# Preparing combined weights on another engine, and sooner, in a fused attention and two-FFN kernel

## The chip, the cores and the metric

The kernel runs on one core of a Trainium2 chip. The metric is the device time of one launch in microseconds (us), the median of three runs. Details come from one further execution that was taken with the hardware profiler.

## What is computed

Three stages follow each other, and the tokens of all four batches are handled as one list of 2304.

```python
# q, k, v: 4 batches, 8 heads, 576 positions, 64 wide
scores = (q @ k.T) / 8 * Dmat          # Dmat[i, j] = gamma_h ** (i - j) for i >= j, else 0
x = scores @ v                         # 2304 x 512
h = x @ w_in                           # 512 -> 2048
g = maximum(h, 0) + alpha * minimum(h, 0)
x = g @ w_out                          # 2048 -> 512
gate = 1 / (1 + exp(-(x @ w_gate)))    # 512 -> 1536
out = (gate * (x @ w_val)) @ w_out2    # 1536 -> 512
```

The weights arrive as 64-bit floating point words; the kernel turns them into 32-bit numbers itself.

## The kernel before

**Products.** Each 32-bit operand is split into a high part (rounded to the fp32r type that TensorE takes) and a low rest, and a product is the sum of three matmuls: high by high, high by low, low by high (`products`, L634 is its matmul). Splitting is a copy on ScalarE and a subtraction on VectorE (`split`, L201 and L202).

**Blocks and stages.** The tokens are cut into blocks of 256, 512, 512, 512 and 512 (j = 0 to 4). TensorE's instructions keep the order in which the program writes them. The other engines' order, and that of the DMA queue on SyncE (SP), which issues every transfer, is made by a planner that simulates the program and places an instruction when the simulation has it ready; `behind` only keeps some work behind marked urgent instructions. Once built, every engine and the queue work strictly by that list.

1. To about 156 us: attention of blocks 0 and 1 with the first FFN on them. The weights of each of the 16 feature chunks f are loaded, made single and split (`prepare_weight`), and written back to HBM; chunks below `RES` stay in SBUF until block 2 has used them, later ones are fetched again (`fetch`, L268).
2. 156 to about 327 us: the loop at the end of the program with j = 1 (its chunks 11 to 15) and j = 2 (chunks 0 to 15), called steps here. Each step is `ffn1_h` (12 matmuls of 512 columns; then ScalarE forms the positive part and the negative part, L648 and L649, VectorE joins them, L650, and `split` follows), and one step later `ffn1_y`. The h results lie in a ring of two PSUM banks (`ps_h`), free again only after the split on VectorE. Between them run the attention of blocks 2 to 4, chunk of tokens by chunk (`att_stages`: scores, a mask on VectorE at L519, values; GpSimd scales the next chunk's q and v, L497 and L505), and preparations of the second FFN's weights.
3. 327 to about 410 us: blocks 3 and 4 together in four double steps (`h_step`). Two chunks and their partners eight chunks on are computed with seven half-size products instead of eight. This needs combinations of the tokens (`seven`, tiles `xx_1` to `xx_7`, made in `left_factors(-1)` during the last steps of j = 2) and of the weights: the **sums**, `prepare_sums(t)` for t = 0 to 7, two for each double step. `leaky` (L760, L761, L763) makes the activation of a double step.
4. 410 to 505 us: `y_phase`. From there to the end the second FFN runs in the same seven-product form, then block 0 in plain form.

**Preparations.** A list `jobs` holds 18 preparations of the second FFN's weights (`prepare_quarters`). One loads two raw tiles, makes them single (ScalarE L224, L225; VectorE L228, L230, L233), combines quarters on GpSimd (L300), splits them (ScalarE L310, VectorE L311) and writes them to HBM. `ask` loads the raw tiles of the next one, if two of five raw slots are free; `begin_job` starts it; `second_pace(n)` adds n to a count in each step of the loop, asks at one half and begins at one. `second_step` moves every running preparation on by one piece. `begin_job((1, t))` puts a sum at the head of the list; but if some other preparation is already asked for, that one is started and the sum waits for the next call. In the program before, step 12 of j = 2 calls it for sum 0 with a preparation asked for.

A sum reads the tile `b` (two weight tiles written to HBM earlier, L367) and is three subtractions on GpSimd (L336: one of 128 x 512, two of 128 x 256), a copy on ScalarE (L344) and a subtraction on VectorE (L346).

**SBUF.** Everything else lies in 38 slots of 4 KB per partition, handed out in the order in which they came free: 5 are raw slots, the other 33 hold weights, activations, attention chunks (a q and k slot, a k and v slot) and the halves of preparations. In step 12 of j = 2 seven of them are set aside for the weights of the double steps (`load_inner`).

Of the kernel before, what the change touches and what calls it, by code (L numbers as in the profile page):

```python
# [10 lines left out]
F32 = mybir.dt.float32  # L11
# [4 lines left out]
ALU = mybir.AluOpType  # L16
# [3 lines left out]
P = 128  # L20
# [3 lines left out]
DM = 512  # L24
KC = DM // P
NF1 = 2048 // P
# [17 lines left out]
PLAIN = 3  # L44
# [1 line left out]
NIN = NSUM // 2  # L46


RES = 10


EARLY, LATE = 2, 5
# [1 line left out]
BESIDE = 11  # L54
# [9 lines left out]

PACE_S, PACE_Y = 0.33, 0.5


SPAN_X = 21  # L70


def chunks():
# [39 lines left out]
def retention_two_ffn(ctx: ExitStack, tc: tile.TileContext, att, cst, alpha, w1, w2, out0, out1):  # L113
    nc = tc.nc
# [217 lines left out]
    def prepare_sums(t):  # L332

        b, s = raw_w.pop((1, t))
        b21, b22 = b[:, 0, DM // 2:], b[:, 1, DM // 2:]
        sub = lambda o, a, b: nc.gpsimd.tensor_tensor(out=o, in0=a, in1=b, op=ALU.subtract)  # L336
        sub(s[:, 0:2], b[:, 1].rearrange("p (k j) -> p k j", k=2), b[:, :, :DM // 2])
        yield
        sub(s[:, 2], b22, s[:, 0])
        sub(s[:, 3], b21, s[:, 2])  # L340
        free(b)
        yield
        w = [slot([P, 4, DM // 2], F32R, f"s{t}{x}", quarter_slots) for x in "hl"]
        nc.scalar.activation(w[0], s, AF.Copy)  # L344
        yield
        nc.vector.tensor_tensor(out=w[1], in0=s, in1=w[0].bitcast(F32), op=ALU.subtract)  # L346
        free(s)
        inner[t // 2, t % 2, 0] = w
# [5 lines left out]
    asked = []  # L354
# [12 lines left out]
                nc.sync.dma_start(out=b, in_=w1f[t])  # L367

    def begin_job(*now):
        jobs[:0] = now  # L370
        ask()
        if asked:
            job = asked.pop()
            second.append((job, (prepare_sums, prepare_quarters)[job[0] - 1](*job[1:])))
# [19 lines left out]
    def second_pace(n):  # L394
        second_step()
        due[0] += n
        if due[0] >= 1.0:
            due[0] -= 1.0
            begin_job()
        elif due[0] >= 0.5:  # L400
            ask()
# [34 lines left out]
    def weight_step(n):  # L436

        credit[0] += n
        if credit[0] >= 1.0:
            credit[0] -= 1.0  # L440
            begin_weight()
        advance()
# [4 lines left out]
    o = 0  # L447
# [4 lines left out]
    def load_chunk(n):  # L452
        if n >= len(CHUNKS) or n in raw_a:
            return
        load_qk(n)
        load_kv(n)

    def load_qk(n):
        if n >= len(CHUNKS):
            return  # L460
        c = CHUNKS[n][3]
        half = 2 * c * H * D
        qk = slot([P, 2, NPAIR, P], F32, f"qk{n}")
        a = offset[n]
        src = att[a:a + half].rearrange("(p t a i) -> p t a i", p=P, t=2, a=NPAIR)
        if n == 0:
            nc.sync.dma_start(out=c_sb, in_=cst)
            nc.sync.dma_start(out=qk[:, :, 0:2, :c], in_=src[:, :, 0:2])
            nc.sync.dma_start(out=qk[:, :, 2:4, :c], in_=src[:, :, 2:4])
        else:  # L470
            nc.sync.dma_start(out=qk[:, :, :, :c], in_=src)
        raw_a[n] = [qk, None]

    def load_kv(n):
        if n >= len(CHUNKS):
            return
        c = CHUNKS[n][3]
        half = 2 * c * H * D
        kv = slot([P, 2, H * D], F32, f"kv{n}")
        a = offset[n] + half  # L480
        nc.sync.dma_start(out=kv[:c], in_=att[a:a + half].rearrange("(p t d) -> p t d", p=c, t=2))
        raw_a[n][1] = kv

    x_t = {}
    def att_q(n):

        _, _, pos, c, _ = CHUNKS[n]
        by = decay
        if pos:

            by = ap.tile([P, NPAIR, P], F32, tag="dec", name=f"dec{n}", bufs=2)
            for pr in range(NPAIR):
                g = O_GP + STARTS.index(pos) * NPAIR + pr
                nc.scalar.activation(by[:, pr, :c], decay[:, pr, :c], AF.Copy, scale=c_sb[:, g:g + 1])
        for part in (slice(0, 2), slice(2, 4)) if n == 0 else (slice(0, 4),):
            q = raw_a[n][0][:, 0, part, :c]
            nc.gpsimd.tensor_tensor(out=q, in0=q, in1=by[:, part, :c], op=ALU.mult)  # L497
# [83 lines left out]
    def att_stages(j):  # L581

        for n in runs_of(j):
            x_of(n)
            s_sb = att_scores(n, ps_a, "ab")
            load_qk(n + 1)
            yield
            att_values(n, s_sb, ps_a, "ab")
            load_kv(n + 1)
            if n + 1 < len(CHUNKS):  # L590
                att_q(n + 1)
                att_v(n + 1)
            yield
# [78 lines left out]
    def ffn1_y(j, f):  # L672
        w, g = weight(f, 1), g_t.pop((j, f))
        if f == 0:
            if j == 0:
                y_t[j] = [t[:, e] for t in [
                    ps_a.tile([P, 2, BLOCKS[j]], F32, tag=x, name=f"y{j}{x}") for x in "ab"
                ] for e in range(2)]
            else:
                y_t[j] = [ps_y.tile([P, BLOCKS[j]], F32, tag="y", name=f"y{j}_{e}") for e in range(KC)]  # L680
        for e in range(KC):

            products(
                y_t[j][e], [(cols(w, e), g)],
                f == 0 and (j > 0 or e % 2 == 0), f == NF1 - 1 and (j > 0 or e % 2 == 1),
            )
        used(f, 1)
        free(g)
        if f == NF1 - 1:
            for e in range(KC):  # L690
                drain(e, f"yst{j}_{e}", y_t[j][e], x2d[j][:, e, :])
# [64 lines left out]
                yield  # L756

    def leaky(dst, src, f, name):
        t = small.tile([P, DM], F32, tag="t", name=name, bufs=1)
        nc.scalar.activation(t, src, AF.Relu)  # L760
        urgent["act"].append(nc.scalar.activation(src, src, AF.Relu, scale=-1.0))  # L761
        urgent["dve"].append(
            nc.vector.scalar_tensor_tensor(dst, src, na_sb[:, f:f + 1], t, ALU.mult, ALU.add)  # L763
        )
# [397 lines left out]
    for f in range(NF1):  # L1162

        while step1 < EARLY or (step1 - EARLY) * (NF1 - 1) < (BESIDE - EARLY) * f:
            ffn1_h(1, step1)
            weight_step(PACE_C)
            later(BEHIND - 1 if step1 >= EARLY else EARLY)
            late.append((1, step1))
            step1 += 1
            if step1 > EARLY:  # L1170
                break
        ffn1_y(0, f)
        weight_step(PACE_C)
        weight_step(PACE_C)
        if done[0] < NF1:
            ffn1_h(0, done[0])
            done[0] += 1
        weight_step(PACE_C)
        weight_step(PACE_C)
    n = runs_of(2)[0]  # L1180
    load_chunk(n)
    att_q(n)
    att_v(n)
    def stages_of(*js):
# [3 lines left out]
    for j in range(1, PLAIN):  # L1188
        stages = stages_of(2) if j == 1 else stages_of(3, 4)
        first = step1 if j == 1 else 0  # L1190
        total = 2 * sum(len(runs_of(i)) for i in ((2,) if j == 1 else (3, 4)))
        span = SPAN * (NF1 - first) // NF1 if j == 1 else SPAN_X
        staged = 0
        for f in range(first, NF1):
            fetch(f, 0)
            fetch(f + 1, 0)
            fetch(f, 1)
            ffn1_h(j, f)
            second_pace(PACE_S)
            if j == PLAIN - 1 and staged == total:  # L1200
                if not under_left:

                    for _ in stages:
                        pass
                    for x in "ab":
                        ps = ps_a.tile([P, DM], F32, tag=x, name=f"whole{x}")
                        nc.tensor.matmul(ps, wt[f, 1][:, 0, :P], x_t[j][:, 0, 0], start=True, stop=True)
                    att_only.close()
                    pool = ctx.enter_context(tc.tile_pool(name="late", bufs=1, reuse_waits="tile"))
                    spare.extend((pool, f"late{i}") for i in range(NLATE))  # L1210
                    under_left.append(left_factors(-1))
                else:
                    next(under_left[0], None)
            if j == PLAIN - 1 and f == 12:
                quarter_slots.extend(spare.popleft() for _ in range(NQ))
                load_inner(0)
            if j == PLAIN - 1 and f in (12, 13):
                begin_job((1, f - 12))
            for point in range(2):
                second_step()  # L1220
                if staged < total and staged * span < total * (2 * (f - first) + point):
                    next(stages)
                    staged += 1
                if point == 0:
                    later(BEHIND - 1)
                elif under_left:
                    next(under_left[0], None)
            late.append((j, f))
        for _ in stages:
            pass  # L1230
# [168 lines left out]
```

## Time and profile before

| | |
|---|---|
| Median of 3 runs | 904.96 us (903.76 to 906.84) |
| The profiled execution | 906.68 us |
| Its span, first to last instruction | 904.9 us |
| Mean granted clock of TensorE | 0.991 |
| TensorE matmul (PE) busy | 862.4 us, 95% |
| VectorE (DVE) busy | 564.9 us, 62% |
| ScalarE (ACT) busy | 447.4 us, 49% |
| GpSimd (POOL) busy | 152.0 us, 17% |
| Chain that ended last | PE 67%, DVE 13%, DMA 8%, ACT 6%, issue 3%, SP's queue 2%, POOL 1% |

A busy share is time in which an instruction of that engine ran. The chain that ended last is followed back from the last instruction, at each step to what released it. "A <- B" in the lists of waits says that A sat idle until B ended.

### The profile page before, as it was taken

The page shows a single profiled execution, that of the slowest core. Times are in us where ns is not written, and L with a number is a line of the kernel's source. Part 1 is how long each engine was busy: PE and PEld are TensorE (multiplying, and loading weights), DVE is VectorE, ACT ScalarE, POOL GpSimd, SP SyncE. Part 2 cuts the span into 40 slices and gives each one's busy share as a digit, 9 for nine tenths or more (in the row PEclk, how much of TensorE's full clock was granted, in tenths as well). Part 3 has the DMA queues.
Part 4 walks back from the last instruction along what each step waited for, and adds up shares of the span by engine and source line. Part 5 has one row for each costly group of instructions (what it writes and reads, how often), then busy time and mean ns, then how long its engine had stood idle before and what let it go on. Part 6 is the DMA issues. An engine that isn't in the chain of part 4 may idle for free.

```text
span 904.9 us, 13084 instructions
## 1 busy us (share of the span) xinstructions
PE 862.4 (95%) x4770; PEld 719.3 (79%) x4770; DVE 564.9 (62%) x805; ACT 447.4 (49%) x785; POOL 152.0 (17%) x143
## 2 busy tenths in 40 slices
PE   5689989999999989999999999999999999999998
PEld 4578978777778867777788888887888888888897
DVE  2689995475665976776984877358952233497122
ACT  3478884445543675676752655335532322353111
POOL 5100001233621742321440231100000000000000
PEclk9799999999999999999999999999999999999999
DMA  9679998776785845669698799934598554269970
GB/s 296 231 256 352 370 391 319 269 248 245 246 319 212 337 178 177 227 232 339 224 401 338 257 399 418 409 144 163 194 378 334 188 185 163 97 208 349 395 278 24
DMA packets 89392, 244.01 MB, mean 270 GB/s; under 512 B 13040, under 2 KB 16112, under 8 KB 89328
## 3 DMA queue, kind: packets, MB, share of 16 engines
q1 hardware_dynamic: 89328, 243.17, 74.1%
q8 instruction: 38, 0.62, 0.3%
q14 instruction: 26, 0.21, 0.1%
HBM read 174.98 MB, written 68.16 MB: 269 GB/s over the span
## 4 chain that ended last, share of the span: by engine, by line
PE 67%; DVE 13%; DMA 8%; ACT 6%; issue 3%; SPq 2%; POOL 1%; DVEq 0%; ACTq 0%; POOLq 0%
PE a L634 14%; PE oa L634 7%; PE yy L634 7%; PE h L634 5%; PE y L634 5%; PE z L634 4%; PE e L634 4%; PE b L634 4%; PE c L634 3%; PE o L634 2%; PE oc L634 2%; PE ob L634 2%; PE oe L634 2%; DMA kv<-att 2%; PE a_h L634 2%
## 5 line engine op out<-in xcount | busy, mean ns | idle before, releaser
L634 PE MATMUL h<-x,w 128*128 128x512 f32 (+1 forms) x444 | 89.6, 353 | 5.8 <-DVE g L202 4.3
L634 PEld LDWEIGHTS h<-x,w 128*128 128x128 f32 x444 | 71.0, 192 | 18.1 <-DVE g L202 5.7
L300 POOL TENSOR_TENSOR r<-r,r 128x256 f32<-128x256 f32 x36 | 43.2, 1206 | 165.7 <-DVE r L233 111.6
L311 DVE TENSOR_TENSOR q<-r,q 128x512 fp32r<-128x512 f32 x72 | 54.2, 783 | 17.7 <-ACT q L310 17.5
L634 PE MATMUL y<-g,w 128*128 128x512 f32 x252 | 61.8, 394 | 0.0
L310 ACT ACTIVATE q<-r 128x512 fp32r<-128x512 f32 x72 | 46.2, 668 | 25.2 <-POOL r L300 16.6
L634 PEld LDWEIGHTS y<-g,w 128*128 128x128 f32 x252 | 46.6, 188 | 10.7 <-issue 1.0
L650 DVE SCALAR_TENSOR_TENSOR h<-h,na_sb,t 128x512 f32<-128x512 f32 (+1 forms) x48 | 31.9, 665 | 34.1 <-ACT h L649 34.0
L648 ACT ACTIVATE t<-h 128x512 f32<-128x512 f32 (+1 forms) x48 | 25.1, 522 | 55.5 <-PE h L634 55.3
L224 ACT ACTIVATE r<-r 128x512 f32<-128x512 f32 x68 | 45.6, 670 | 13.6 <-DMA r<-w 13.6
L960 DVE TENSOR_TENSOR c<-a,es 128x512 f32<-128x512 f32 x24 | 16.7, 697 | 52.6 <-PE a L634 52.4
L225 ACT ACTIVATE r<-r 128x512 int32<-128x512 uint32 x68 | 45.5, 669 | 0.0
L497 POOL TENSOR_TENSOR qk<-qk,dec 128x512 f32<-128x512 f32 (+1 forms) x16 | 18.9, 1182 | 152.5 <-DMA kv<-att 123.3
L233 DVE SCALAR_TENSOR_TENSOR r<-r 128x512 uint32<-128x512 uint32 x52 | 39.3, 763 | 0.4
L230 DVE CUSTOM_DVE_ANT_0 r<-r,top 128x1024 uint16<-128x1024 uint16 x52 | 37.0, 726 | 1.9 <-ACT r L225 0.2
L201 ACT ACTIVATE g<-h 128x512 fp32r<-128x512 f32 (+1 forms) x48 | 25.1, 522 | 24.7 <-DVE h L650 24.6
L634 PEld LDWEIGHTS z<-x,zp 128*128 128x128 f32 x288 | 36.0, 192 | 0.9
L515 PE MATMUL s<-qk 64*128 64x128 f32 (+1 forms) x320 | 23.6, 288 | 13.4 <-POOL qk L497 6.7
L634 PE MATMUL z<-x,zp 128*128 128x256 f32 x288 | 36.3, 283 | 0.0
L515 PEld LDWEIGHTS s<-qk 64*128 64x128 f32 (+1 forms) x320 | 19.6, 190 | 19.6 <-POOL qk L497 7.0
L300 POOL TENSOR_TENSOR r<-r 128x256 f32<-128x256 f32 x36 | 33.0, 920 | 11.0 <-DVE r L233 7.3
L202 DVE TENSOR_TENSOR g<-h,g 128x512 fp32r<-128x512 f32 (+1 forms) x48 | 28.6, 597 | 9.7 <-ACT g L201 9.3
(460 smaller groups left out, 2286.3 us busy)
## 6 DMA issues: line engine op xcount, KB each, us to landing
tq<-td SPq DMA_DIRECT2D x84, 512.0 KB, 9.3
r<-w SPq DMA_DIRECT2D x68, 512.0 KB, 6.4
wo<-wod SPq DMA_DIRECT2D x42, 512.0 KB, 3.9
v<-w1d SPq DMA_DIRECT2D x38, 512.0 KB, 5.9
td<-q SPq DMA_DIRECT2D x36, 512.0 KB, 4.4
w1d<-w SPq DMA_DIRECT2D x32, 512.0 KB, 5.8
wod<-q SPq DMA_DIRECT2D x24, 512.0 KB, 10.1
zp<-td SPq DMA_DIRECT2D x48, 256.0 KB, 5.2
```

Of the source, the lines that this page charges most:

```text
L201: a = nc.scalar.activation(hi, src, AF.Copy)
L202: d = nc.vector.tensor_tensor(out=lo, in0=src, in1=hi.bitcast(F32), op=ALU.subtract)
L224: nc.scalar.activation(high.bitcast(F32), high.bitcast(F32), AF.Copy, scale=2.0 ** -112)
L225: nc.scalar.activation(low.bitcast(I32), low, AF.Copy, scale=2.0 ** -29)
L230: nc.vector.tensor_tensor(out=out.bitcast(I32), in0=low.bitcast(I32), in1=top.bitcast(I32), op=ALU.add)
L233: nc.vector.scalar_tensor_tensor(out, high, 0x80000000, out, ALU.bitwise_and, ALU.bitwise_or)
L300: sub = lambda o, a, b: nc.gpsimd.tensor_tensor(out=o, in0=a, in1=b, op=ALU.subtract)
L310: nc.scalar.activation(part[0], src, AF.Copy)
L311: nc.vector.tensor_tensor(out=part[1], in0=src, in1=part[0].bitcast(F32), op=ALU.subtract)
L515: nc.tensor.matmul(ps[e][:c, pr, :c], qk[r, 1, pr, :c], qk[r, 0, pr, :c], start=True, stop=True)
L634: nc.tensor.matmul(ps, l, r, start=first and i == 0, stop=last and i == len(todo) - 1, skip_group_check=joins)
L650: nc.vector.scalar_tensor_tensor(ps, ps, na_sb[:, f:f + 1], t, ALU.mult, ALU.add)
```

## The change

- The three subtractions of a sum go to VectorE.
- `UNTIL` is 9: the seven slots are set aside, `load_inner(0)` runs and the first two sums are called for in steps 9 and 10 of j = 2, not 12 and 13. A preparation that is already asked for is started at once, and the sum is begun in the same call. From step 9 on the loop's own `second_pace` is left out; up to there its pace is 0.4 and not 0.33.
- `leaky` takes its positive part from the tag "s", which has two buffers, and not from "t", which has one.
- The loads of an attention chunk are written two chunks ahead, not one.
- `RES` is 9: chunk 9's two weight tiles no longer stay for block 2 and are fetched again. Chunk 11's first tile is fetched earlier.

```diff
-RES = 10
+RES = 9
-PACE_S, PACE_Y = 0.33, 0.5
+PACE_S, PACE_Y = 0.4, 0.5
+UNTIL = 9
 def prepare_sums(t):
-        sub = lambda o, a, b: nc.gpsimd.tensor_tensor(out=o, in0=a, in1=b, op=ALU.subtract)
+        sub = lambda o, a, b: nc.vector.tensor_tensor(out=o, in0=a, in1=b, op=ALU.subtract)
 def begin_job(*now):
+        while now and asked:
+            begin_job()
         jobs[:0] = now
 def att_stages(j):
-            load_qk(n + 1)
+            load_qk(n + 2)
...
-            load_kv(n + 1)
+            load_kv(n + 2)
 def leaky(dst, src, f, name):
-        t = small.tile([P, DM], F32, tag="t", name=name, bufs=1)
+        t = small.tile([P, DM], F32, tag="s", name=name)
...
         ffn1_y(0, f)
+        if f == NF1 - 2:
+            fetch(BESIDE, 0)
...
     load_chunk(n)
+    load_chunk(n + 1)
...
             ffn1_h(j, f)
-            second_pace(PACE_S)
+            if j < PLAIN - 1 or f < UNTIL:
+                second_pace(PACE_S)
...
-            if j == PLAIN - 1 and f == 12:
+            if j == PLAIN - 1 and f == UNTIL:
...
-            if j == PLAIN - 1 and f in (12, 13):
-                begin_job((1, f - 12))
+            if j == PLAIN - 1 and UNTIL <= f < UNTIL + 2:
+                begin_job((1, f - UNTIL))
```

## Rows read from the trace of the kernel before

**Rows 1.** Windows: busy us (instructions) of PE, PEld, DVE, ACT, POOL; PE clock, DMA share, GB/s.

```profile
156.00:235.00 79.00, 76.20 (x589) 61.62 (x588) 44.55 (x75) 38.20 (x82) 23.83 (x24) 1.00 0.77 253
235.00:290.00 55.00, 53.23 (x428) 42.77 (x427) 35.47 (x57) 23.77 (x47) 19.19 (x19) 1.00 0.75 273
290.00:332.00 42.00, 37.69 (x173) 30.46 (x172) 38.87 (x40) 27.84 (x43) 24.00 (x18) 0.96 0.71 263
332.00:410.00 78.00, 75.67 (x328) 60.62 (x327) 52.38 (x74) 51.55 (x92) 23.89 (x24) 1.00 0.60 204
410.00:440.00 30.00, 28.04 (x120) 21.91 (x118) 22.87 (x28) 24.27 (x39) 4.64 (x3) 1.00 0.80 295
440.00:850.00 410.00, 408.56 (x1800) 337.65 (x1801) 244.01 (x295) 169.20 (x243) 38.05 (x34) 1.00 0.74 276
```

**Rows 2.** Waits of PE: who waited for whom, us in total, times, longest us.

```profile
PE o L534 <- DVE qk L519: 3.2, 3, 1.8
...
PE e_h L634 <- DVE g L763: 2.1, 4, 0.8
```

**Rows 3.** PE in order of time, 296 to 340 us: start, us, instruction, [idle before].

```profile
318.30 3.01 PE L634 MATMUL h<-x,v 128*128 128x512 f32 x12 [0.91 <-DVE g L202]
...
327.43 0.50 PE L634 MATMUL a_h<-xx_1h,wi 128*128 128x512 f32 x1 [3.39 <-DVE g L202]
...
331.88 2.91 PE L634 MATMUL y<-g,v 128*128 128x512 f32 x12
```

**Rows 4.** VectorE in order of time, 285 to 335 us.

```profile
311.86 2.32 DVE L346 TENSOR_TENSOR s0l<-s,s0h 128x1024 fp32r<-128x1024 f32 x1
...
323.23 1.75 DVE L202 TENSOR_TENSOR xx_6l<-xx_s,xx_6h 128x1024 fp32r<-128x1024 f32 x1
324.90 0.75 DVE L650 SCALAR_TENSOR_TENSOR h<-h,na_sb,t 128x512 f32<-128x512 f32 x1
...
331.96 1.21 DVE L346 TENSOR_TENSOR s2l<-s,s2h 128x1024 fp32r<-128x1024 f32 x1
```

**Rows 5.** Groups by shape, 290 to 335 us: busy us, mean ns, idle before.

```profile
L336 POOL TENSOR_TENSOR s<-b,s 128x256 f32<-128x256 f32 x8 | 11.2, 1411 | 0.5
L311 DVE TENSOR_TENSOR q<-r,q 128x512 fp32r<-128x512 f32 x8 | 7.9, 1042 | 0.0
L336 POOL TENSOR_TENSOR s<-b 128x512 f32<-128x512 f32 x4 | 7.6, 1898 | 5.8 <-issue 5.8
...
L230 DVE CUSTOM_DVE_ANT_0 r<-r,top 128x1024 uint16<-128x1024 uint16 x2 | 1.7, 844 | 0.1
L228 DVE TENSOR_SCALAR top<-r 128x512 uint32<-128x512 uint32 x2 | 1.4, 686 | 0.0
L233 DVE SCALAR_TENSOR_TENSOR r<-r 128x512 uint32<-128x512 uint32 x2 | 1.4, 677 | 0.0
```

**Rows 6.** Groups by shape on VectorE, the whole span.

```profile
L202 DVE TENSOR_TENSOR g<-h,g 128x512 fp32r<-128x512 f32 x32 | 21.9, 686 | 8.1 <-ACT g L201 7.8
...
L202 DVE TENSOR_TENSOR g<-h,g 128x256 fp32r<-128x256 f32 x16 | 6.7, 418 | 1.5 <-ACT g L201 1.5
```

**Rows 7.** ScalarE in order of time, 405 to 430 us.

```profile
422.44 0.60 ACT L760 ACTIVATE lt<-a_h 128x512 f32<-128x512 f32 x1 [0.88 <-DVE g L763]
...
424.40 0.60 ACT L760 ACTIVATE lt<-a_h 128x512 f32<-128x512 f32 x1 [0.88 <-DVE g L763]
```

**Rows 8.** GpSimd in order of time, 258 to 264 us.

```profile
260.12 1.43 POOL L497 TENSOR_TENSOR qk<-qk,dec 128x512 f32<-128x512 f32 x1 [12.33 <-DMA qk<-att]
```

**Rows 9.** VectorE in order of time, 262 to 271 us.

```profile
265.14 0.69 DVE L311 TENSOR_TENSOR q<-r,q 128x512 fp32r<-128x512 f32 x1 [3.04 <-ACT q L310]
...
269.69 0.68 DVE L519 TENSOR_TENSOR sc<-s,c_sb 128x512 f32<-128x512 f32 x1
```

**Rows 10.** DMA issues, 235 to 332 us: count, KB each, median us to landing.

```profile
v<-w1d SPq DMA_DIRECT2D x12, 512.0 KB, 7.1
```

**Rows 11.** Waits of all engines.

```profile
POOL s L336 <- DMA b<-w1f: 22.7, 2, 12.8
```

## The prediction

> **What bounds the kernel now.** I read the windows of busy time first. From 440 us on TensorE is busy for 408.56 of 410 us [rows 1]: nothing is to be won there, and all that the change touches there is the number of things prepared beforehand. Up to 156 us the change only moves one load, so what is left are the five windows from 156 to 440. Their TensorE idle times are the window less its busy time: 2.80, 1.77, 4.31, 2.33 and 1.96 us, 13.2 in sum. In the third one VectorE is busy for 38.87 of 42 us and the granted clock is 0.96 [rows 1], so that window has another engine as its bound; in the others VectorE stands at 56 to 76% and TensorE's stops are short ones with particular causes.
>
> The waits of TensorE name the causes [rows 2]: in the attention the masked scores (L519), in the double steps the activation's last instruction on VectorE (L763). The timeline shows the third window's stops: 0.91 us ahead of the last h group at 318.3, and 3.39 us ahead of the first product of the double steps at 327.4 [rows 3]. Both wait for VectorE's split of an h result (L202), which frees one of the two banks that h results take. So it is not the new factors that are late but the old work, which stands in VectorE's list among the new.
>
> After the longer stop TensorE runs slower for a while: the twelve matmuls from 327.43 to 331.88 take 4.45 us, and the twelve of the same shape behind them 2.91 [rows 3]. [...] This costs 1.5 us more. What the change can win at most is therefore 13.2 + 1.5 = 14.7 us.
>
> **The change part by part.**
>
> *Hand-over to the double steps (sums on VectorE, begun sooner, no other preparations).* VectorE's load between 290 and 335 us has three parts to be moved or removed. First, preparations: eight splits L311 (7.9 us) and the making of singles for two raw tiles (1.7 + 1.4 + 1.4 us) [rows 5], 12.4 us. By the code's counts, before, one preparation begins under j = 1, four in steps 1, 4, 7 and 10 of j = 2, the sixth in step 12, and a seventh is asked for in step 14. After, two begin under j = 1, three in steps 2, 4 and 7, the sixth in step 9, and none follows until the first double step. That makes the same six before the hand-over, and the last two lie three steps sooner. Second, slow instructions: while GpSimd works on the sums, a 128 x 1024 subtraction took 2.32 us, and 1.21 with GpSimd idle [rows 4]. Five splits of that size from 311.86 to 323.23 were stretched (2.32, 1.75, 2.32, 1.76 and 1.75 us, first and last in [rows 4]), to 9.9 us against 5 x 1.21: 3.9 us. Third, against that, the sums themselves arrive. One subtraction of 128 x 512 at 0.69 and two of 128 x 256 at 0.42 us [rows 6] make 1.52 us a sum, 12.2 us for all eight; GpSimd needs 1.90 + 2 x 1.41 us for one here [rows 5]. Up to four sums fall into this window, 6.1 us, or two (3.0) if the first two lie some four steps sooner. Net: 12.4 + 3.9 - 6.1 = 10.2 us less for VectorE at least, against 4.3 us by which it is late; the L650 at 324.9 [rows 4], which is the late one, belongs to the h group before that at 318.3. On SP's queue the two `b` loads and the six of `load_inner` go three to four steps sooner, past fetched weights and the writes of preparations, at a DMA share of 0.75 [rows 1]; a quarter of that time is free, so I cost this within the last part below. I take 5.3 of the 5.8 us (4.31 idle, 1.5 clock). Bounds: 0, if something else holds the bank, and 5.8.
>
> [...]
>
> *Positive parts in two buffers.* At 422 to 424 us one `leaky` follows the next at 1.96 us (424.40 less 422.44). ScalarE works for 1.08 of that, and then stands 0.88 us until VectorE has read the only buffer [rows 7]. With two buffers the next pair of ScalarE instructions runs meanwhile, and the pace is ScalarE's 1.08 us. Six in a row end about 5 us sooner, and in pairs of two about 0.9 us sooner. The stops of the double steps that wait for them are 0.8 us at the longest [rows 2], and those of the y phase lie in the 1.96 us of its window [rows 1]. So most of 2.33 + 1.96 = 4.3 us goes. What is late next is VectorE's list, which now holds two sums for each of three double steps (3.0 us of 20), less what GpSimd's sums stretched there. One stop near 440 us is a split in the y phase and stays. I take 3.8. Bounds 1.5 and 4.3; tag "s" is free there, since its other users are the attention and the second FFN.
>
> *Attention loads two chunks ahead.* GpSimd stood 12.33 us for one q and k load [rows 8]. Its list is strict, so the quarter combinations behind that scaling came late too; ScalarE's and VectorE's splits of them came late (VectorE idle 3.04 us), and the mask, which stands behind these, began only at 269.69 [rows 9], with TensorE waiting. This is the pattern of the longer two of the three L519 waits, 3.2 us in sum [rows 2]. The two windows lose 2.80 + 1.77 = 4.6 us together, and 2.7 is what I take: the mask's place behind the splits remains, and there is one more preparation before step 9. Bounds: -2 and 4.6.
>
> *Chunk 9 fetched again, chunk 11 sooner.* Two more loads of 512 KB, 7.1 us each to landing [rows 10], on a queue whose engines are 75% and 71% busy [rows 1]. They hide behind the steps 8 and 9 of j = 2; the two slots they free pay for the two that the attention chunk takes. If that cover goes, one load of 7.1 us less a step's two groups of twelve matmuls (2 x 2.91 [rows 3]) is a stop of 1.3. Together with the denser preparations I put 0.5 us for this, bounds 0 and 4. The earlier load of chunk 11 meets no stop at 156 us and is costed at nothing, hidden by the matmuls of the blocks 0 and 1; without that cover it would be another 1.3 us.
>
> Sum: 5.3 + 3.8 + 2.7 - 0.5 = 11.3 us. The profiled execution took 906.68 us (span 904.9), 1.72 more than the median, and would come to 895.4. Against the median of 904.96 it is **893.7 us**.
>
> **The rivals.**
>
> *The crowd moves instead of going (898 us).* Three preparations and two sums now lie in steps 4 to 10, among the attention. The window from 235 to 290 goes from 35.5 us of VectorE [rows 1] to some 45 of 55, by a preparation more (half of the 12.4 us above) and two sums. The masks then stand behind more splits: the attention wins nothing (2.7) and loses some 1.5, 893.7 + 4.2 = 897.9. For it: a mask has no mark of urgency. Against: GpSimd's long waits were the start of the two long stops.
>
> *The sums are not begun sooner (899 us).* The planner orders by its own simulation, and it had the first sums and their loads well ahead of where the program writes them. If the hand-over stays as crowded, its 5.3 us stay away: 899.0. Against: the 12.4 us of preparations are moved by the program's order.
>
> *All is given back (904 us).* More slot traffic, denser preparations and weights that come late cost some 10 us in small stops between 156 and 290. It takes six or seven stops of 1.5 us more; L519 has three in all now [rows 2].
>
> *VectorE stands for a load (908 us).* GpSimd waited 22.7 us for the tile `b` of two sums, 12.8 at the longest [rows 11], and nobody cared. The same wait in VectorE's list holds the activations and splits behind it, and with them the banks that TensorE needs. VectorE is idle for a third of the double steps [rows 1], so of 22.7 us some 15 would show, 893.7 + 15 = 908.7. It decides from where `b` lands more than a group's 2.91 us after VectorE reaches the sum. Against: the planner gave GpSimd those sums early because GpSimd was empty; on VectorE there is other work to place first. [...]
>
> **How the numbers follow.** Forecast 0.58, the crowd moves 0.15, sums not sooner 0.10, all given back 0.09, VectorE stands 0.08. The lower end is all bounds at their best, 904.96 - 14.7 = 890.3, less some 2.8 for refills of TensorE's pipeline, which no idle time shows: 887.5. The upper end takes in the two rivals at 898 and 899 with 3 us for their own spread, 902.5, and leaves out 0.17 above and little below. A difference within 0.3% (2.7 us) can't be told from none here. Faster by more than that, below 902.2: 0.83; within it 0.09; slower 0.08.
>
> **What would show it.** Right: in the windows, VectorE well below 90% in the 40 us before the first double step; no stop over 1 us and a granted clock of 1.00 there; sums (L336) on VectorE at 0.4 to 0.7 us and the 1024-wide splits near 1.21; ScalarE's waits for L763 (ahead of L760) nearly gone; GpSimd's waits for q and k loads short. Wrong: waits of VectorE on `b` of microseconds; TensorE's waits on L519 longer than 3.2 us or on a fetched weight; a new stop at the hand-over by another releaser, such as the load of the inner weights.

## The result and the profile after

The changed kernel takes **891.2 us** (median; 889.66 to 891.92) against 905.31 for the kernel before in the same comparison: ratio 0.984 (0.982 to 0.986), 14.1 us faster. The forecast was 893.7, with a range of 887.5 to 902.5.

The page of the changed kernel, its first lines and the chain that ended last:

```profile
span 889.1 us, 13072 instructions
PE 856.2 (96%) x4770; PEld 716.7 (81%) x4770; DVE 566.2 (64%) x829; ACT 446.6 (50%) x785; POOL 126.5 (14%) x119
PE 50%; DMA 5%; DVE 2%; ACT 2%; issue 1%; SPq 0%; ACTq 0%; DVEq 0%
```

The trace follows this chain back only to 350.56 us, so its shares make up 60% of the span and can't be set against those of the kernel before, whose chain reaches back to the start. VectorE is no less busy in all (566.2 against 564.9 us): it took over the sums, and its work lies elsewhere. To see where the time went, I read the start of certain TensorE groups in both timelines and take their differences. In us:

| Stretch | before | after | difference |
|---|---|---|---|
| Start to block 1's first h group | 49.2 | 47.2 | -2.0 |
| to block 1's chunk 11 | 107.0 | 107.0 | 0.0 |
| attention: to step 9 of block 2 | 121.4 | 120.6 | -0.8 |
| steps 9 to 12 | 23.2 | 23.3 | +0.1 |
| hand-over: step 12 to the second double step | 52.8 | 46.2 | -6.5 |
| to the y phase | 61.3 | 58.5 | -2.9 |
| y phase | 90.9 | 87.0 | -3.8 |
| second FFN to the end | 399.1 | 399.2 | +0.1 |

The first line is scatter of the first loads (see the second profile of the kernel before, below). The other lines make 13.8 us; the medians differ by 14.1.

The windows answer to [rows 1]; the third one covers the same work as 290 to 332 us before, and the following ones are shifted likewise:

```profile
156.00:235.00 79.00, 76.44 (x587) 61.26 (x586) 55.58 (x86) 43.83 (x93) 30.23 (x29) 1.00 0.85 291
235.00:290.00 55.00, 54.31 (x447) 43.62 (x446) 37.50 (x62) 26.08 (x49) 17.73 (x18) 1.00 0.83 306
283.00:325.00 42.00, 42.00 (x212) 34.64 (x211) 29.23 (x37) 23.05 (x37) 0.00 (x0) 1.00 0.57 201
325.00:400.00 75.00, 75.00 (x330) 61.55 (x329) 60.29 (x92) 56.02 (x99) 11.79 (x12) 1.00 0.64 222
400.00:430.00 30.00, 29.48 (x130) 24.08 (x130) 26.92 (x34) 23.65 (x36) 12.97 (x6) 1.00 0.92 342
```

At the hand-over TensorE is never idle, its granted clock is 1.00, and VectorE is busy for 29.23 of 42 us, where it was 38.87. GpSimd does nothing. VectorE's load stands elsewhere now: 55.58 us in the first window, 11 more than before (twelve splits of preparations, L312, against eight), and 60.29 of 75 us in the double steps against 52.38 of 78.

TensorE in order of time at the hand-over, as in [rows 3], and its waits, as in [rows 2]:

```profile
314.53 2.88 PE L637 MATMUL h<-x,v 128*128 128x512 f32 x12
...
319.97 0.39 PE L637 MATMUL a_h<-xx_1h,wi 128*128 128x512 f32 x1
```

```profile
PE o L537 <- DVE qk L522: 1.2, 3, 0.6
...
PE a_h L637 <- DVE g L865: 0.5, 1, 0.5
```

No stop is left ahead of either group, and the first double step's twelve products take 2.72 us, from 319.97 to the next group's start at 322.69, where they took 4.45. Of the waits for a `leaky` none is left (L865 is the addition of two results). The masks (L522 now) still hold TensorE three times, but for 1.2 us in all.

VectorE in order of time at the hand-over, as in [rows 4], and the waits of ScalarE for `leaky`, after and (last line) before:

```profile
306.96 1.23 DVE L203 TENSOR_TENSOR xx_5l<-xx_s,xx_5h 128x1024 fp32r<-128x1024 f32 x1 [1.13 <-ACT xx_5h L202]
...
311.64 1.28 DVE L337 TENSOR_TENSOR s<-b 128x512 f32<-128x512 f32 x2
...
315.11 0.42 DVE L337 TENSOR_TENSOR s<-b,s 128x256 f32<-128x256 f32 x1
```

```profile
ACT lt L763 <- DVE g L766: 2.6, 4, 1.4
```

```profile
ACT lt L760 <- DVE g L763: 19.7, 19, 3.0
```

The wide splits take 1.22 us each, the sums' subtractions 0.68 (the row above merges two) and 0.42. ScalarE waited 19.7 us for the single buffer in the kernel before and waits 2.6 now. Between 156 and 290 us GpSimd waits 13.5 us for q and k loads, where it waited 36.5.

### The profile page after: what moved, and what is told of

It reads as the page before. It is cut to its first block, busy times and chain, and to the rows that moved or that the text cites. A ratio compares the mean times of both kernels' runs of the same rounds, so it can differ in the third digit from the quotient of the medians.

```text
span 889.1 us, 13072 instructions
## 1 busy us (share of the span) xinstructions
PE 856.2 (96%) x4770; PEld 716.7 (81%) x4770; DVE 566.2 (64%) x829; ACT 446.6 (50%) x785; POOL 126.5 (14%) x119
## 4 chain that ended last, share of the span: by engine, by line
PE 50%; DMA 5%; DVE 2%; ACT 2%; issue 1%; SPq 0%; ACTq 0%; DVEq 0%
PE a L637 13%; PE yy L637 10%; PE oa L637 7%; PE z L637 4%; PE e L637 3%; DMA r<-w 3%; PE b L637 3%; PE c L637 3%; PE o L637 2%; PE oc L637 2%; PE ob L637 2%; PE oe L637 2%; DMA tq<-td 1%; DMA wo<-wod 1%; DVE q L312 0%
## 5 line engine op out<-in xcount | busy, mean ns | idle before, releaser
L637 PE MATMUL h<-x,w 128*128 128x512 f32 (+1 forms) x432 | 85.5, 348 | 7.6 <-DVE g L203 5.8
L637 PEld LDWEIGHTS h<-x,w 128*128 128x128 f32 x432 | 67.6, 189 | 19.5 <-DVE g L203 7.3
L301 POOL TENSOR_TENSOR r<-r,r 128x256 f32<-128x256 f32 x36 | 46.1, 1288 | 242.7 <-DVE r L234 196.7
L312 DVE TENSOR_TENSOR q<-r,q 128x512 fp32r<-128x512 f32 x72 | 54.6, 784 | 16.2 <-ACT q L311 15.9
L311 ACT ACTIVATE q<-r 128x512 fp32r<-128x512 f32 x72 | 46.2, 671 | 28.7 <-POOL r L301 17.9
L637 PE MATMUL y<-g,w 128*128 128x512 f32 x240 | 58.9, 394 | 0.0
L225 ACT ACTIVATE r<-r 128x512 f32<-128x512 f32 x68 | 45.6, 670 | 15.7 <-DMA r<-w 15.6
L637 PEld LDWEIGHTS y<-g,w 128*128 128x128 f32 x240 | 44.4, 188 | 10.2 <-issue 1.0
L234 DVE SCALAR_TENSOR_TENSOR r<-r 128x512 uint32<-128x512 uint32 x52 | 37.4, 724 | 0.5
L637 PE MATMUL h<-x,v 128*128 128x512 f32 x144 | 35.4, 395 | 0.0
L637 PE MATMUL y<-g,v 128*128 128x512 f32 x144 | 35.2, 393 | 0.0
L518 PE MATMUL s<-qk 64*128 64x128 f32 (+1 forms) x320 | 23.3, 285 | 12.3 <-POOL qk L500 7.3
```

Of the source, the lines that this page charges most:

```text
L225: nc.scalar.activation(high.bitcast(F32), high.bitcast(F32), AF.Copy, scale=2.0 ** -112)
L234: nc.vector.scalar_tensor_tensor(out, high, 0x80000000, out, ALU.bitwise_and, ALU.bitwise_or)
L311: nc.scalar.activation(part[0], src, AF.Copy)
L312: nc.vector.tensor_tensor(out=part[1], in0=src, in1=part[0].bitcast(F32), op=ALU.subtract)
L637: nc.tensor.matmul(ps, l, r, start=first and i == 0, stop=last and i == len(todo) - 1, skip_group_check=joins)
```

## The experiments

All times are medians, beside runs of the kernel before on the same chip. "Attention", "hand-over", "double steps" and "y phase" are the stretches of the table, read from each run's own timeline.

### Undoing one part of the changed kernel

**The sums back on GpSimd.**

```diff
-        sub = lambda o, a, b: nc.vector.tensor_tensor(out=o, in0=a, in1=b, op=ALU.subtract)
+        sub = lambda o, a, b: nc.gpsimd.tensor_tensor(out=o, in0=a, in1=b, op=ALU.subtract)
```

> The changed kernel with the sums' three subtractions back on GpSimd, all else as changed. Theory 1 (VectorE's list: the hand-over was late because preparations stood in VectorE's list among the activations; moving them sooner is what freed it): the hand-over stays clear, the sums on GpSimd stretch some VectorE splits by about 4 us that now have slack; 891.5 to 893.5 us, no stop over 1 us ahead of the first double step. Theory 2 (the engine: GpSimd's sums holding up VectorE's two-input instructions was what made it late, so the move of the sums to VectorE is what freed it): part of the 0.9 and 3.4 us stops come back, 894 to 897 us.

Measured: 893.01 us, ratio to before 0.986 (0.982 to 0.990). The hand-over takes 46.2 us, as in the changed kernel, and TensorE has no stop there. The windows, and a split of VectorE's that is stretched while GpSimd works on a sum:

```profile
283.00:325.00 42.00, 42.00 (x212) 34.87 (x210) 27.16 (x30) 23.93 (x36) 6.36 (x6) 1.00 0.61 212
```

```profile
291.99 2.27 DVE L347 TENSOR_TENSOR s1l<-s,s1h 128x1024 fp32r<-128x1024 f32 x1 [0.18 <-ACT s1h L345]
```

The hand-over stays clear, as theory 1 has it. But this does not rule out theory 2. Begun sooner, the four sums ahead of the first double step end on GpSimd at 295.7 us, 23 us before it, and GpSimd works for 6.36 us of this window, where it was 24.00 [rows 1]. Only this one wide split is stretched. So the sooner start took the stretching away together with the preparations. What this run loses lies in the double steps, 60.7 us against 58.5. There ScalarE's list stood for 4.29 us behind the raw tile of a preparation, with the activations behind it:

```profile
386.29 0.67 ACT L225 ACTIVATE r<-r 128x512 f32<-128x512 f32 x1 [4.29 <-DMA r<-w]
...
387.41 0.60 ACT L763 ACTIVATE lt<-a_h 128x512 f32<-128x512 f32 x1
```

Whether that comes from the engine or only from the other list, no run shows.

**The sums late again, with preparations beside them** (steps 12 and 13, pace 0.33; all the rest as changed).

```diff
-PACE_S, PACE_Y = 0.4, 0.5
+PACE_S, PACE_Y = 0.33, 0.5
...
-        while now and asked:
-            begin_job()
...
-            if j < PLAIN - 1 or f < UNTIL:
-                second_pace(PACE_S)
+            second_pace(PACE_S)
...
-            if j == PLAIN - 1 and f == UNTIL:
+            if j == PLAIN - 1 and f == 12:
...
-            if j == PLAIN - 1 and UNTIL <= f < UNTIL + 2:
-                begin_job((1, f - UNTIL))
+            if j == PLAIN - 1 and f in (12, 13):
+                begin_job((1, f - 12))
```

> The changed kernel with the sums begun from step 12, pace 0.33, and preparations up to the end of block 2 as in the kernel before; sums on VectorE. Theory 1 (VectorE's list): the stops at the hand-over come back with the lower clock behind them, 5 to 7 us, 896 to 898 us, and VectorE over 90% busy in the 40 us before the first double step. Theory 2 (the engine): sums on VectorE suffice, no stop over 1 us at the hand-over, 891 to 893 us.

Measured: 892.82 us, 0.986 (0.982 to 0.991). The hand-over takes 47.3 us, 1.1 more than in the changed kernel and 5.4 less than before. Its windows, and what is left of the long stop:

```profile
283.00:325.00 42.00, 41.12 (x206) 33.58 (x205) 37.88 (x54) 27.08 (x43) 7.68 (x8) 1.00 0.63 221
```

```profile
PE a_h L635 <- DVE g L203: 0.8, 1, 0.8
```

Theory 1 expected the stops to come back, and they did not. VectorE is 90% busy, nearly as in the kernel before, and yet the stop is 0.8 us: a full list alone does not make it. Here theory 2 holds. Either edit is enough to free the hand-over, and both leave GpSimd little to do there (7.68 us here).

**One buffer for the positive part.**

```diff
-        t = small.tile([P, DM], F32, tag="s", name=name)
+        t = small.tile([P, DM], F32, tag="t", name=name, bufs=1)
```

> The changed kernel with leaky's positive part back in the single buffer t. Theory 1: the stops in the double steps and at the start of the y phase come back, ScalarE's waits of 0.88 us with them: 4 to 7 us, 895 to 898 us, all of it between the first double step and the second FFN. Rival (those stops went because GpSimd no longer stretches VectorE's instructions there): the stops stay away, 891 to 892.5 us.

Measured: 899.4 us, 0.992 (0.990 to 0.995), 8 us more than the changed kernel and above the expected 898. Double steps 63.5 us (58.5 changed, 61.3 before), y phase 89.3 (87.0). The waits:

```profile
PE e_h L637 <- DVE g L766: 2.4, 4, 1.1
PE e_h L637 <- ACT hes L851: 2.1, 1, 2.1
```

```profile
ACT lt L763 <- DVE g L766: 16.7, 18, 2.1
```

The rival falls: the sums are on VectorE here, and the stops are back. With the sums in VectorE's list a single buffer costs more than it did before the change (8.2 us here, 5.6 below).

**Attention loads one chunk ahead.**

```diff
-            load_qk(n + 2)
+            load_qk(n + 1)
...
-            load_kv(n + 2)
+            load_kv(n + 1)
...
-    load_chunk(n + 1)
```

> The changed kernel with attention loads one chunk ahead again (chunk 9 still fetched again). The time from block 1's first h group to step 9 of block 2 was 0.8 us shorter in the changed kernel than before. Theory 1 (the loads give that little because the masks stay behind the splits): 891 to 893 us, and GpSimd's long waits for q and k loads come back. Rival (the loads give the 2.7 us of the forecast or more, hidden by a cost of the denser preparations): 894 to 897 us.

Measured: 893.66 us, 0.987 (0.983 to 0.990). The attention takes 125.3 us, 4.7 more than in the changed kernel; that is the rival's side, though the median differs by only 2.5 and lies between the two expectations. GpSimd's long waits for q and k loads come back in part (9.7 and 7.5 us, against 8.0 and 5.3). The attention's largest stop is a new one: the scores stood behind GpSimd's quarter combinations, which share GpSimd's list with the scaling of q.

```profile
225.29 2.08 PE L518 MATMUL s<-qk 64*128 64x128 f32 x16 [2.58 <-POOL r L301]
```

### One part alone on the kernel before

**Two buffers.** The `leaky` line of the change alone.

```diff
-        t = small.tile([P, DM], F32, tag="t", name=name, bufs=1)
+        t = small.tile([P, DM], F32, tag="s", name=name)
```

> The kernel before with one edit: leaky's positive part in two buffers. Putting it back to one buffer in the changed kernel cost 7 to 8 us between the first double step and the second FFN. Theory 1 (the single buffer alone made those stops): 4.5 to 6.5 us faster than before, 899 to 901 us, the hand-over stops unchanged. Rival (the stops also need the sums off GpSimd): 1 to 3 us faster, 902.5 to 904.5 us.

Measured: 899.84 us, 0.994 (0.991 to 0.996), 5.6 us faster than before. Double steps 59.8, y phase 87.0; the hand-over's long stop stays, 3.3 us. As expected by theory 1. The clock behind that stop stays at 1.00 in this profile (0.996 in the mean of the execution, 0.991 before), and the hand-over takes 51.1 us, 1.7 less than before.

**Sums on VectorE.**

```diff
-        sub = lambda o, a, b: nc.gpsimd.tensor_tensor(out=o, in0=a, in1=b, op=ALU.subtract)
+        sub = lambda o, a, b: nc.vector.tensor_tensor(out=o, in0=a, in1=b, op=ALU.subtract)
```

> The kernel before with one edit: the sums' subtractions on VectorE, begun as late as before, among the preparations. In the changed kernel either undoing alone left the hand-over nearly clear, so each of the two may suffice. If the engine suffices: the hand-over (step 12 to the second double step) is 4 to 6 us shorter; but with the single buffer the double steps lengthen by some 2 us; 900 to 903 us. If it does not suffice alone: the hand-over stops stay above 3 us in sum; 904 to 908 us.

Measured: 903.06 us, 0.998 (0.996 to 1.000). Hand-over 47.3 (5.4 less), double steps 65.6 (4.3 more), y phase 89.3 (1.6 less). The move to VectorE is enough at the hand-over and loses most of that again with one buffer: twice the expected 2 us in the double steps, and a time just above the expected 903. VectorE's window and its groups there, as in [rows 1] and [rows 5]:

```profile
290.00:332.00 42.00, 41.22 (x196) 33.84 (x195) 37.92 (x51) 28.82 (x45) 6.72 (x7) 1.00 0.73 258
```

```profile
L311 DVE TENSOR_TENSOR q<-r,q 128x512 fp32r<-128x512 f32 x8 | 5.5, 733 | 0.0
```

VectorE is busy for 37.92 us and was for 38.87: the sums came in, the stretching went out (the eight L311 splits from 1042 to 733 ns, too). In the two kernels' lists, the activation's L650 of steps 13 and 14 each stands one wide split earlier, and the wide split of sum 1 falls behind L650 of step 15. So it was not VectorE's busy time that made the h results late, but the order of its list and what the stretching added to it; this run does not part these two.

**Sums sooner, no preparations beside them.** The `UNTIL` lines, the pace and the loop in `begin_job` alone.

```diff
+        while now and asked:
+            begin_job()
...
+            if j < PLAIN - 1 or f < UNTIL:
+                second_pace(PACE_S)
...
```

> The kernel before with one edit: the sums from step 9, pace 0.4, no preparation begun from step 9 on; sums on GpSimd, one buffer, loads one chunk ahead. If the moved preparations suffice: the hand-over is 5 to 7 us shorter. The denser preparations with loads one chunk ahead cost up to 4 us in the attention, as they did in the changed kernel with loads one ahead: 900 to 904 us. If they do not suffice: hand-over stops above 3 us, 905 to 909 us.

Measured: 903.27 us, 0.998 (0.996 to 1.000). Hand-over 46.2, and the double steps as before, 61.4. But the attention takes 126.4 us, 4.9 more: the pace of 0.4 gives most of the hand-over's 6.6 us back there. The time is as expected. Here too GpSimd's sums end 23 us before the first double step (at 301.1 us; before, they ended at 323.9, 3.5 us before it).

**Loads two chunks ahead, with chunk 9's slots.**

```diff
-RES = 10
+RES = 9
...
-            load_qk(n + 1)
+            load_qk(n + 2)
...
-            load_kv(n + 1)
+            load_kv(n + 2)
...
+    load_chunk(n + 1)
```

> The kernel before with one edit: attention loads two chunks ahead, paid for with chunk 9's slots. Theory of the forecast (loads that come late start the stops at the masks): 2 to 4 us faster, 901 to 903.5 us. Rival (at the old pace the loads do not decide; the masks' place in VectorE's list does): within 1.5 us of before, 904 to 906.5 us.

Measured: 908.4 us, 1.003 (1.002 to 1.005), 3 us slower than before; both expectations missed. The attention takes 125.8 us, 4.3 more. The loads came sooner: GpSimd's waits for loads between 156 and 290 us fall from 67 to 41 us, and the two longer stops at the masks (1.83 us at 220.0, 1.19 at 271.1 before) are gone. But other stops came in, and one place has most of the loss, in TensorE's order of time and in ScalarE's:

```profile
182.97 2.08 PE L515 MATMUL s<-qk 64*128 64x128 f32 x16 [2.62 <-issue]
184.98 4.99 PE L634 MATMUL h<-x,v 128*128 128x512 f32 x12
```

```profile
177.73 1.28 ACT L494 ACTIVATE dec<-c_sb 128x128 f32<-128x128 f32 x4 [1.52 <-POOL qk L497]
178.91 0.58 ACT L201 ACTIVATE g<-h 128x512 fp32r<-128x512 f32 x1
179.39 0.66 ACT L224 ACTIVATE r<-r 128x512 f32<-128x512 f32 x1
...
181.02 0.65 ACT L225 ACTIVATE r<-r 128x512 int32<-128x512 uint32 x1
181.56 0.58 ACT L201 ACTIVATE x<-o 128x512 fp32r<-128x512 f32 x1
```

By the program the scores wait for a bank that the split `x<-o` frees (the trace names no releaser; VectorE's half of that split ends at 182.87). It stands in ScalarE's list behind a scaling table (L494) and a preparation's four conversions. In the kernel before only the conversions stood there, and the stop was 0.8 us. A second new stop, 1.68 us at the masks at 165.4, hangs on a load and on the list: GpSimd waits 6.36 us for q and k, ScalarE's L494 waits 3.42 us for GpSimd, and the activation's split stands behind L494, where it stood ahead of it before. So the loads land sooner, and the planner made another list of it.

### What makes the attention's stops

**The kernel before once more,** for a second profile.

> The kernel before once more, unchanged, for a second profile. The first block 1 group began at 49.2 us in its profile, and at 45.7 to 49.1 in nine others, though no edit touches the first 50 us. If that is scatter of the first loads: it begins anywhere from 45 to 49 us here, and the stretches behind it (attention 121.4 us to step 9 of block 2, hand-over 52.8, double steps 61.3, y phase 90.9) agree within 1 us each with the first profile.

Measured: 908.02 us, one run. Block 1's first h group began at 45.9 us; the stretch behind it took 109.0 us (107.0), the attention 122.3 (121.4), the hand-over 54.1 (52.8), double steps 61.3, y phase 90.9. So the first 50 us scatter (45.6 to 49.2 us over all fourteen profiles), and the 2.0 us of the table's first line are no gain of the change. The hand-over missed its 1 us: more of it ran at the lower clock (0.57 from 326 to 334 us, 0.79 in the first profile).

**Preparations behind the attention's work.**

```diff
             for point in range(2):
-                second_step()
                 if staged < total and staged * span < total * (2 * (f - first) + point):
                     next(stages)
                     staged += 1
+                second_step(0)
```

`second_step(0)` passes `ahead=0` to `behind`.

> The changed kernel; in the loop over block 1 and 2 a piece of a preparation is written behind the attention's piece and must stand behind the last urgent instruction, not the last but two. In ScalarE's list the making of singles then no longer stands ahead of the split that frees the scores' banks. Theory (stops in the attention come from where ScalarE's and VectorE's lists put preparations, and the loads only shuffle that): the stretch from block 1's chunk 11 to step 9 of block 2, 120.6 us in the changed kernel, gets 2 to 4 us shorter; 887 to 889.5 us. Rival (loads and slots set it): 890.5 us or more, with GpSimd waiting for loads as long as now.

Measured: 890.55 us, 0.983 (0.980 to 0.986), not to be told from the changed kernel. The attention takes 120.0 us, 0.7 less. The stop at the scores is gone and block 1's part is 2.4 us shorter, but block 2's is 1.7 longer, with new stops of about 1 us at the masks and at the attention's state. By its time this is the rival's outcome, and GpSimd waits for loads as long as in the changed kernel (33 us between 156 and 290, against 32). So the order of the lists moves the stops, and this order is no better on the whole; that the order alone makes them, this run does not show.

**Half the preparations in the attention.**

```diff
-PACE_S, PACE_Y = 0.4, 0.5
+PACE_S, PACE_Y = 0.2, 0.5
```

> The changed kernel with pace 0.2 instead of 0.4: half the preparations in the attention's stretch, the others later, in the second FFN, where TensorE has had no stop but DMA is at a share of 1.0 for some 60 us. Theory (preparations in the lists make the attention's stops): that stretch gets 2 to 4 us shorter and nothing is lost later, 887 to 889.5 us. Rival (the later part can't take them): the stretch gets shorter, but stops on loads appear behind 490 us; 890 to 896 us.

Measured: 906.82 us, 1.001 (1.000 to 1.004); both times expected were missed. The attention takes 116.7 us, 3.9 less than in the changed kernel; TensorE is idle for 0.38 us of the window from 156 to 290:

```profile
156.00:235.00 79.00, 78.72 (x613) 64.08 (x612) 41.98 (x69) 37.88 (x87) 27.11 (x27) 1.00 0.71 241
235.00:290.00 55.00, 54.90 (x440) 44.81 (x439) 32.41 (x56) 22.46 (x40) 9.11 (x10) 1.00 0.65 227
490.00:570.00 80.00, 80.00 (x354) 66.30 (x354) 55.18 (x87) 45.47 (x79) 19.11 (x21) 1.00 1.03 408
```

GpSimd waits longer for loads there than in the changed kernel (41 us against 32), so a late load alone does not make these stops. And the run loses four times that gain in one stop:

```profile
PE a L637 <- DVE p L979: 17.1, 1, 17.1
```

The program begins all that is left of the list in the fourth step of the second FFN, and VectorE's L979 stands behind it. DMA is at its full share for the 80 us ahead, but so it is in the changed kernel (1.01).

**The same, with the rest in the y phase.**

```diff
-PACE_S, PACE_Y = 0.4, 0.5
+PACE_S, PACE_Y = 0.2, 0.7
```

> The changed kernel with pace 0.2 in the attention's stretch, as in the slow-pace run, and 0.7 instead of 0.5 in the y phase, so that by the code's counts 12 of 18 preparations have begun when the second FFN starts (13 in the changed kernel, 10 in the slow-pace run, which made up for it at once at 580 us with a stop of 17 us). Theory (the attention's stops come from preparations among its work, and the y phase has room): the attention's stretch keeps the slow pace's 116.7 us, 3.9 less than in the changed kernel, and no stop appears at 580 us; 886.5 to 889 us. Rival (the y phase, where VectorE is over 90% busy in its first 30 us, or the second FFN's DMA at a share of 1.0 can't take it): the stops come back behind 400 us; 890 us or more.

Measured: 906.98 us, 1.000 (0.998 to 1.003). The attention keeps its 116.8 us, but stops of 6.4 and 6.5 us appear in the y phase and in the second FFN:

```profile
PE a L637 <- DVE p L979: 6.5, 1, 6.5
PE yy L637 <- DMA v<-w1d: 6.4, 1, 6.4
```

From 560 to 600 us the queue's packets take 99.0% of the 16 engines' time (51% in the changed kernel):

```profile
q1 hardware_dynamic: 4472, 15.35, 99.0%
```

So the preparations are what stops the attention: with half of them it is 3.9 us shorter in both runs. Whether by their place in the lists or by their transfers (the DMA share of the first window falls from 0.85 to 0.71), the runs don't part. Both ways of putting them off cost more behind 400 us than they won. No version among these beats the changed kernel by more than its scatter.

## Why the prediction was right, point by point

**The hand-over** was given 5.3 us and measured 6.5; the lower clock behind the stop went with it. (Against the other three profiles that keep the stop it is 4.9 to 7.9, mostly by what the clock did behind it.) That VectorE loses 10.2 us of work in the 40 us ahead came near: 38.87 to 29.23 us, 9.6. Its parts did not, and that they cancel is luck. Four splits of a preparation (2.6 us) still lie there, and two masks (1.4); two sums came in (3.0), not four; and six wide splits had been stretched there, by 4.5 us, not five by 3.9.

The account itself was the weaker step: it took the preparations, the stretching and the sums as one load of VectorE. The runs show two remedies that are each enough: sooner alone gives 46.2 us, sums on VectorE alone 47.3, both together 46.2. With the second VectorE is as full as before, so its load alone does not make the stop. And the two have one effect in common: they take GpSimd's sums, and with them the stretching, out of the last 23 us before the first double step. No run moves the preparations and keeps the stretching, so the preparations' share in the stop stays open, and so does that of the list's order.

**Two buffers** were given 3.8 us with an upper bound of 4.3, and the double steps and the y phase gave 6.7 (2.9 + 3.8); alone, the edit gives 5.3 there (1.5 + 3.8) and 5.6 in the median. This is the term that was mis-sized. The mechanism is shown: ScalarE's wait fell from 19.7 to 2.6 us and all stops for L763 went, and with one buffer they come back. The bound was read from idle time, and a stop costs more than that. In the y phase, where the table has 3.8 us, the kernel before has three stops with 2.6 us of idle time, the last of them the split near 440 us that I left standing and that went as well:

```profile
PE yy L634 <- DVE g L763: 1.7, 2, 1.0
...
PE yy L634 <- DVE g_00l L202: 0.9, 1, 0.9
```

And at 359 us it has 0.67 us idle, but 1.06 us lie between two matmul starts that are otherwise 0.23 apart, 0.83 lost:

```profile
357.94 0.40 PE L634 MATMUL e_h<-xx_5h,s2l 128*128 128x512 f32 x1
359.00 0.50 PE L634 MATMUL e_h<-xx_5h,s3h 128*128 128x512 f32 x1 [0.67 <-DVE g L763]
```

**Loads two ahead, chunk 9, denser preparations** were given 2.7 - 0.5 = 2.2 us, and the attention gave 0.8, which is within scatter: in three other profiles whose edits don't touch it, it takes 120.7 to 122.9 us. The step that failed is that loads that land sooner take the stops at the masks away and put none in their place. One of the two stops that the prediction traced to late loads fits [rows 8] [rows 9]. Ahead of the other, at 220.0 us, GpSimd had waited only 1.4 us for a load, and four splits of a preparation stood before the mask in VectorE's list. Alone, the loads took both stops away and still made the kernel 3 us slower, by new stops of 1.68, 2.62 and 1.19 us where the engines' lists came out otherwise. The changed kernel needs the loads because it has the denser pace: without them its attention takes 4.7 us more. Whether they help there by landing sooner or by the other list that they lead to, no run parts.

**The sum** was right to 2.8 us of 14.1, because two terms too small (by 1.2 and 2.9 us) and one too large (by 1.4) stood in it; that they nearly cancel is luck. And the edits don't add: alone they give -5.6, -2.4, -2.2 and +3.0, which is -7.1, and together -14.1 (chunk 11's earlier load, in none of the four, was not run alone). Some edits make others worth more: the sums on VectorE lengthen the double steps by 4.3 us with one buffer and not with two, and the pace costs 4.9 us in the attention with loads one ahead and nothing with two. The 2.8 us for refills in the range's lower end stood on no row, and no run shows them; what the runs show beyond idle time is the 0.16 us at 359 us and 1.2 in the y phase.

**The rivals.** "VectorE stands for a load" did not come: VectorE waited for `b` once, for 0.5 us.

```profile
  DMA b<-w1f: 0.5, 1
```

Its mechanism is real, on ScalarE: the 4.29 us for a raw tile above, with activations behind it, made a stop of about 2 us. "The crowd moves" came half true: it moved to 156 to 235 us (VectorE 44.55 to 55.58 us), not to 235 to 290 (35.47 to 37.50), and with loads one ahead the attention is 4.7 us longer. "The sums are not begun sooner" fell: the first sum's subtraction begins at 264.7 us, against 295.4 on GpSimd before. "All is given back" came in part with each of two edits alone: the attention is 4.9 us longer with the sums sooner and 4.3 with the loads, against the rival's 10.

## What to carry to other kernels

When an engine that works through a fixed list is full just ahead of a hand-over, look which old instruction stands among the new ones in its list, what frees the bank it holds, and which instructions take longer than elsewhere while another engine works (here a wide split of VectorE's, 2.27 us during a sum on GpSimd against 1.22). Two remedies can each be enough, and the second then adds nothing; ask what they have in common before naming the cause. Price a stop from the distance of matmul starts, not from idle time. Edits that share an engine's list don't add: test them in pairs, since an edit that loses alone (loads two ahead) may be what lets another one pay.

## What the runs showed of the hardware that was not expected

Whether TensorE's clock falls behind a stop could not be told from the stop's length. With one buffer in the changed kernel two stops that cost 1.3 and 2.3 us within 4 us left the clock at 1.00; with the sums alone on VectorE, it was 0.83 over the 10 us with stops of 1.3 and 3.0 us at the same place; and behind one of 2.62 us idle in the attention it was 0.61 over the next 8:

```profile
389.00:399.00 10.00, 6.77 (x29) 4.97 (x28) 6.65 (x11) 7.04 (x15) 2.17 (x3) 1.00 0.74 280
```

```profile
392.00:402.00 10.00, 6.11 (x19) 4.26 (x18) 5.80 (x10) 6.20 (x13) 1.67 (x3) 0.83 0.72 272
```

```profile
183.00:191.00 8.00, 8.00 (x40) 6.66 (x42) 4.99 (x8) 0.94 (x2) 5.28 (x6) 0.61 0.19 69
```

In the last one the scores behind the stop took 2.08 us and the twelve matmuls after them 4.99, where 1.16 and 3.02 are usual, so a stop of 2.62 us cost 5.5.

The hand-over's stop shows it most plainly: it has 3.35 to 3.39 us idle in three profiles of kernels that differ at most in the buffers, and from 326 to 334 us the granted clock is 0.79 in the kernel before, 1.00 with two buffers alone, and 0.57 in the second profile of the kernel before:

```profile
326.00:334.00 8.00, 7.14 (x19) 5.60 (x20) 6.60 (x8) 7.66 (x12) 0.00 (x0) 0.57 0.53 194
```
